# Squares on ScalarE for the upper part; from block 3 on VectorE makes the lower parts, the scalings and w_out's sums in GpSimd's place

## The chip, the cores and the metric

The kernel runs on one core of one Trainium2 chip. The metric is the device time of one execution in microseconds, from first to last instruction with what lies around it. Times below are either the median of several runs or come from one profiled execution, and the text says which.

## What is computed

A retention layer over 4 batches of 768 tokens (8 heads of 64), an MLP of 512 to 2048 to 512 with a squared ReLU, and a routed MLP of 8 experts with 384 tokens each. The inputs are float32.

```python
state = gamma * state + k_t v_t^T            # per head, over the 768 steps
y[t]  = scale * q_t state                     # 3072 tokens x 512 in all
h = x @ w_in
g = s * relu(h)**2 + b
x2 = g @ w_out
logits = x2 @ w_gate                          # 8 experts, 384 tokens each, chosen greedily
out[tokens of e] = relu(x2[tokens of e] @ w1[e]) @ w2[e]
```

The choice of experts depends on the order of the logits, so the kernel keeps more than one float32r pass of precision: each factor of a matmul is split into an upper part (rounded to float32r) and a lower part (the rest), and three products are summed (upper by upper, upper by lower, lower by upper).

## The kernel before

The tokens are cut into 12 blocks of 256 (two chunks of 128 each). The first MLP runs per block in 16 steps f over d_ff. `h_unit` (line 401) makes 12 matmuls of 256 columns into one PSUM bank (2 or 3 in turn), the h bank, and ScalarE copies relu(h) from it into the tile r (L412), which has two buffers. VectorE then multiplies max(h, 0), read from the bank, by r and writes the square in place (L413); only after this is the bank free. `r_split` (L416) has ScalarE round r to the upper part rh (L417) and, on GpSimd, subtracts to get the lower part rl (L418). `x_unit` (L421) makes six matmuls of 512 columns from rh, rl and w_out's parts (L429). `moe1` (L514) issues h units and x units in turn, x two units behind h. At the end of a block `x_out` moves the two result banks to tiles of the pool tmp (L439), which has six buffers.

The order of work on every engine is the order in which the Python code issues it; each engine takes its queue in order. `Weave.unit` (L66) issues a unit and adds its cost to a program time; before each unit it advances the side jobs (generators) whose due time has come. A side job's `yield 900` says that its next piece is due 900 ns later in program time. These numbers only set the order; nothing waits for them on the chip.

There are three stretches before the search for the experts:

- **First stage, blocks 0 to 2 together** (about 50 to 229 us of the trace): 48 units. Beside them `conv_gen` (L233) turns the weights, which come as float64, into upper and lower parts, with five VectorE operations, two ScalarE and two GpSimd operations per tile of 512 columns.
- **Blocks 3 to 9 one by one** (236 to 645 us): 16 h and 16 x units each. Beside block b runs `attn(b + 1)` (L294), the retention of the next block: per chunk `b_part` makes the scores and masks them on VectorE (am, L332), `c_part` makes the output and the next state (L345, L351, L355), ScalarE and VectorE split the output (L363, L364), and the next loads are issued on SyncE's queue. The scalings by powers of gamma (`scale_chunk`, L200: q by qdec, v by vdec) run on GpSimd one chunk ahead. Beside block 9 run the retentions of both blocks 10 and 11, with `PACE` = 0.5 for all due times. `load_dec` and `load_chunk` issue the loads.
- **Blocks 10 and 11 as a pair** (645 to 702 us): `h_pair` (L629) makes both blocks' h and their parts for each f; `l_unit` sums logits from them, and `x_last` makes the x part afterwards.

From block 3 on a further side job, `logits_gen` (L455), makes the logits of finished tokens on VectorE: `gate` (L449) issues eight operations of 512 elements that each multiply a tile by one expert's row and sum it (L452), called gates below. While no finished tile is at hand it does the same to w_out: `const_row` (L474) adds the upper and the lower part into w on GpSimd (L477), adds w to csum, also on GpSimd (L480, L482), and runs eight gates on w. `LG` gives the distance of its pieces, 900 ns of program time. `const_end` (L486) uses csum and the gates' sums once 16 rows are done.

The product that frees the bank and the two parts:

```python
        ACT.activation(r, ph, AF.Relu)
        DVE.scalar_tensor_tensor(r, ph, 0.0, r, op0=OP.max, op1=OP.mult)
        return r

    def r_split(r, rh, rl, eng=POOL):
        ACT.activation(rh, r, AF.Copy)
        eng.tensor_tensor(rl, r, rh.bitcast(F32), op=OP.subtract)
        return rh, rl
```

## Time and profile before

| | |
|---|---|
| median of 3 runs | 1163.41 us (1162.75 to 1167.41) |
| the profiled execution | 1165.52 us, span 1163.8 us |
| TensorE matmul busy | 1029.0 us (88%) |
| VectorE busy | 849.2 us (73%) |
| GpSimd busy | 424.6 us (36%) |
| ScalarE busy | 377.6 us (32%) |
| mean granted TensorE clock | 0.955 of full speed |

The profile comes from one execution; its span is the time between the first and the last recorded instruction. Busy shares are averages over stretches that have different limits, so the busy time is asked for again by stretch. A line such as L452 is a line of the kernel before; PE is TensorE, PEld its weight loads, DVE VectorE, ACT ScalarE, POOL GpSimd and SP SyncE. In the rows of busy time by stretch the columns behind PEclk are the DMA share and GB/s, and (x406) counts instructions. A block's stretch is counted here from the end of the last result copy of the block ahead (L439) to the end of its own; block 3 is counted from 236.00 us, where its first h matmuls begin. In a group's row the idle time before the group's instructions is followed by what ended it.

### The profile page before, as it was taken

How to read it: one execution, taken by the hardware profiler on the slowest of the kernel's cores; microseconds unless marked ns; L12 is line 12 of the kernel's file. 1: busy time of each engine (PE TensorE's matmuls, PEld its weight loads, DVE VectorE, ACT ScalarE, POOL GpSimd, SP SyncE). 2: the span in 40 equal slices, each digit the busy share in tenths (PEclk: the TensorE clock that was granted, in tenths of full speed). 3: DMA queues.
4: the chain of work that ended last, by engine and by line, in shares of the span. 5: the costliest groups of instructions: out<-in, count | busy, mean ns of one | idle time of the engine just before them, and what ended most of it. 6: DMA issues, size and time to landing. Idle time of an engine off the chain costs nothing.

```text
span 1163.8 us, 19793 instructions
## 1 busy us (share of the span) xinstructions
PE 1029.0 (88%) x7636; PEld 881.4 (76%) x7636; DVE 849.2 (73%) x1908; ACT 377.6 (32%) x802; POOL 424.6 (36%) x417
## 2 busy tenths in 40 slices
PE   6887787989999989999999999769789888888997
PEld 5766676878877878878888897657668676777786
DVE  3899999569989888889662724568677787967552
ACT  2333333422323322323232441123333343333442
POOL 3777787733354536454522440010211112021211
PEclk8999989989999999999999999959898999998999
DMA  9322223342212121212130000312333334243440
GB/s 332 128 89 89 96 91 111 111 145 73 65 46 64 46 64 37 74 46 65 47 95 18 20 1 1 136 55 92 118 110 104 108 106 146 79 139 118 160 139 28
DMA packets 35038, 104.50 MB, mean 90 GB/s; under 512 B 4736, under 2 KB 5248, under 8 KB 34944
## 3 DMA queue, kind: packets, MB, share of 16 engines
q1 hardware_dynamic: 30528, 89.60, 23.3%
q0 software_dynamic: 3840, 12.59, 3.3%
q8 instruction: 60, 0.98, 0.3%
q10 hardware_dynamic: 576, 1.05, 0.3%
q14 instruction: 34, 0.28, 0.1%
HBM read 90.64 MB, written 12.58 MB: 89 GB/s over the span
## 4 chain that ended last, share of the span: by engine, by line
PE 44%; DVE 31%; issue 11%; POOL 5%; DMA 5%; ACT 2%; SPq 0%; POOLq 0%; DVEq 0%; ACTq 0%
PE b L409 13%; DVE scr L452 9%; PE b L429 8%; PE b L978 7%; PE b L999 5%; PE b L653 3%; DMA big<-x2d,idx 3%; DVE r L413 3%; DVE tmp L266 3%; DVE tmp L269 2%; DVE tmp L262 2%; DVE l L956 2%; PE b L760 2%; DVE tmp L275 2%; PE b L345 2%
## 5 line engine op out<-in xcount | busy, mean ns | idle before, releaser
L452 DVE SCALAR_TENSOR_TENSOR scr<-tmp,wg 128x512 bf16<-128x512 f32 x288 | 267.3, 928 | 31.5 <-POOL tmp L477 25.1
L409 PE MATMUL b<-xh,h 128*128 128x256 f32 x704 | 205.9, 292 | 32.0 <-DVE r L413 30.3
L418 POOL TENSOR_TENSOR rl<-r,rh 128x256 fp32r<-128x256 f32 x160 | 129.9, 812 | 263.3 <-ACT rh L417 196.0
L409 PE MATMUL b<-xh,l 128*128 128x256 f32 x704 | 201.1, 286 | 0.9 <-POOL l L253 0.9
L409 PE MATMUL b<-xl,h 128*128 128x256 f32 x704 | 200.5, 285 | 0.0
L409 PEld LDWEIGHTS b<-xh,h 128*128 128x128 f32 x704 | 135.6, 193 | 50.6 <-DVE r L413 41.9
L417 ACT ACTIVATE rh<-r 128x256 fp32r<-128x256 f32 x160 | 66.9, 418 | 244.7 <-DVE r L413 244.7
L409 PEld LDWEIGHTS b<-xl,h 128*128 128x128 f32 x704 | 135.8, 193 | 3.7
L413 DVE SCALAR_TENSOR_TENSOR r<-b,r 128x256 f32<-128x256 f32 x192 | 80.4, 419 | 79.5 <-ACT r L412 78.8
L409 PEld LDWEIGHTS b<-xh,l 128*128 128x128 f32 x704 | 136.0, 193 | 1.7 <-POOL l L253 1.5
L429 PE MATMUL b<-h,rh 128*128 128x512 f32 x320 | 130.3, 407 | 5.5 <-ACT rh L417 5.4
L916 POOL DMA_INDIRECT big<-x2d,idx x24 | 26.5, 1103 | 295.2 <-issue 151.4
L429 PE MATMUL b<-h,rl 128*128 128x512 f32 x320 | 127.7, 399 | 3.2 <-POOL rl L418 2.7
L429 PE MATMUL b<-l,rh 128*128 128x512 f32 x320 | 128.8, 402 | 0.0
L412 ACT ACTIVATE r<-b 128x256 f32<-128x256 f32 x192 | 72.5, 378 | 145.5 <-PE b L409 127.5
L978 PE MATMUL b<-gh,h 128*128 128x384 f32 x256 | 94.5, 369 | 0.0
L999 PE MATMUL b<-h,hh 128*128 128x512 f32 x192 | 81.3, 423 | 13.3 <-ACT hh L981 13.3
L978 PE MATMUL b<-gl,h 128*128 128x384 f32 x256 | 89.3, 349 | 0.9 <-DVE gl L928 0.9
L978 PE MATMUL b<-gh,l 128*128 128x384 f32 x256 | 88.6, 346 | 0.0
L956 DVE TENSOR_TENSOR l<-eraw,h 128x512 fp32r<-128x512 f32 x128 | 82.3, 684 | 5.4 <-ACT h L955 5.4
L999 PE MATMUL b<-h,hl 128*128 128x512 f32 x192 | 78.6, 409 | 5.6 <-DVE hl L987 5.4
L999 PE MATMUL b<-l,hh 128*128 128x512 f32 x192 | 77.4, 403 | 0.0
(189 smaller groups left out, 2036.1 us busy)
## 6 DMA issues: line engine op xcount, KB each, us to landing
eraw<-in_w_dram SPq DMA_DIRECT2D x64, 512.0 KB, 3.5
q<-in_qkv_dram SPq DMA_DIRECT2D x36, 512.0 KB, 4.9
raw<-in_w_dram SPq DMA_DIRECT2D x32, 512.0 KB, 3.5
first<-in_qkv_dram SPq DMA_DIRECT2D x24, 256.0 KB, 5.9
qdec<-in_dec_dram SPq DMA_DIRECT2D x24, 256.0 KB, 5.6
x2d<-tmp SPq DMA_DIRECT2D x20, 256.0 KB, 6.1
wg<-in_wgT_dram SPq DMA_DIRECT2D x4, 512.0 KB, 3.8
x2d<-tmp ACTq DMA_DIRECT2D x4, 256.0 KB, 2.0
```

The costliest lines, as they stand in the source:

```text
L266: DVE.scalar_tensor_tensor(ai, hi32, -0x40000000, ai, op0=OP.bitwise_and, op1=OP.bitwise_or)
L409: PE.matmul(ph, a[:, ks], b[:, kc, :], start=(n == 0), stop=(n == 3 * KC - 1))
L412: ACT.activation(r, ph, AF.Relu)
L413: DVE.scalar_tensor_tensor(r, ph, 0.0, r, op0=OP.max, op1=OP.mult)
L417: ACT.activation(rh, r, AF.Copy)
L418: eng.tensor_tensor(rl, r, rh.bitcast(F32), op=OP.subtract)
L429: PE.matmul(X2[blk][t], a[:, ts], b, start=(f == 0 and i == 0), stop=(f == NF - 1 and i == 2))
L452: DVE.scalar_tensor_tensor(scr, x, 1.0, WG[e], op0=OP.mult, op1=OP.mult, accum_out=of[:, e:e + 1])
L653: PE.matmul(XB[c], a[:, cs], b, start=(f == 0 and i == 0), stop=(f == NF - 1 and i == 2))
L956: DVE.tensor_tensor(lo, raw[:, a, :], hi.bitcast(F32), op=OP.subtract)
L978: PE.matmul(PH[0], a[:, ks], b[:, kc, :], start=(kc == 0 and n == 0), stop=(kc == KC - 1 and n == 2))
L999: PE.matmul(Y[i, t], a[:, ts], b, start=(f == 0 and j == 0), stop=(f == NF2 - 1 and j == 2))
```

## The change

**ScalarE squares.** `r_split` now asks ScalarE for Square of r (which holds relu(h)) instead of a copy of the finished square, so the upper part no longer needs VectorE's product. `h_unit` no longer issues that product.

**Blocks 0 to 2.** `r_split` is given the bank `ph`. VectorE's product still reads the bank and still writes r in place, but it is issued behind the Square, which reads the same r, and so it waits for it. GpSimd subtracts as before.

**Block 3 on.** No product reads the bank: ScalarE's Relu alone empties it. `r_split` puts the tiles into the list `LOW`, and `low_parts` issues two VectorE operations of 128x256, r times r in place and then the subtraction. It is called at the next h unit, at the last two x units of a block, and at the end of each `h_pair`.

**Scalings.** In the blocks that are not `wide` (from the retention of block 4 on), `scale_gen` issues the two scalings on VectorE right ahead of the chunk's own scores, 1500 ns of program time apart. Before, GpSimd did it one chunk ahead. The chunks of the retentions issued as `wide` (blocks 0 to 3) keep GpSimd; one of them is the scaling of chunk 8.

**w_out's sums.** `const_row` runs its two additions on VectorE, with one further distance of 900 ns.

**Due times.** A chunk now asks for 3000 for its scalings, 1500 between the two masks, 4500 to `c_part` and 9000 behind it, 18000 in all. `PACE` is gone: the retentions of blocks 10 and 11 beside block 9 have the same distances as the others, where they had half of them.

The places where the order speaks of this are on VectorE. The first is block 4, from the mask products (L332, after the change L344) of chunk 11 on. scr is the output of a gate, wo_s its sum for w_out; before:

```order
L332 TENSOR_TENSOR am<-b_3186,mask 128x512
L332 TENSOR_TENSOR am<-b_3187,mask 128x512
L413 SCALAR_TENSOR_TENSOR r<-b_3199,r 128x256
L452 SCALAR_TENSOR_TENSOR scr,wo_s<-tmp,wg 128x512 x3
L413 SCALAR_TENSOR_TENSOR r<-b_3231,r 128x256
L452 SCALAR_TENSOR_TENSOR scr,wo_s<-tmp,wg 128x512 x3
L413 SCALAR_TENSOR_TENSOR r<-b_3263,r 128x256
L452 SCALAR_TENSOR_TENSOR scr,wo_s<-tmp,wg 128x512 x2
L364 SCALAR_TENSOR_TENSOR xl<-b_3296,xh 128x4x128
L413 SCALAR_TENSOR_TENSOR r<-b_3317,r 128x256
```

After the change:

```order
L344 TENSOR_TENSOR am<-b_3236,mask 128x512
L481 SCALAR_TENSOR_TENSOR scr,wo_s<-tmp,wg 128x512
L344 TENSOR_TENSOR am<-b_3237,mask 128x512
L447 TENSOR_TENSOR r<-r 128x256
L448 TENSOR_TENSOR rl<-r,rh 128x256
L481 SCALAR_TENSOR_TENSOR scr,wo_s<-tmp,wg 128x512
L506 TENSOR_TENSOR tmp<-h_511,l_512 128x512
L511 TENSOR_TENSOR csum<-csum,tmp 128x512
L447 TENSOR_TENSOR r<-r 128x256
L448 TENSOR_TENSOR rl<-r,rh 128x256
L481 SCALAR_TENSOR_TENSOR scr,wo_s<-tmp,wg 128x512 x2
```

The three gates and one product between two units are still three operations of `logits_gen`, of which some are now the sums of w_out (L506, L511), and the product (L413) has become a square and a subtraction (L447, L448).

The second is the end of block 9, from the masks of the last chunk (23) before the change, and from the scaling of v of chunk 22 on after it. L399 and L414 split block 11. Before:

```order
L332 TENSOR_TENSOR am<-b_6409,mask 128x512
L332 TENSOR_TENSOR am<-b_6410,mask 128x512
L413 SCALAR_TENSOR_TENSOR r<-b_6428,r 128x256
L413 SCALAR_TENSOR_TENSOR r<-b_6469,r 128x256
L413 SCALAR_TENSOR_TENSOR r<-b_6495,r 128x256
L413 SCALAR_TENSOR_TENSOR r<-b_6521,r 128x256
L399 TENSOR_TENSOR xl<-tmp,xh 128x512 x2
```

After the change:

```order
L204 TENSOR_TENSOR q_6085<-q_6085,vdec 128x512
L344 TENSOR_TENSOR am<-b_6477,mask 128x512
L344 TENSOR_TENSOR am<-b_6478,mask 128x512
L201 TENSOR_TENSOR q_6352<-q_6352,qdec 128x512
L204 TENSOR_TENSOR q_6354<-q_6354,vdec 128x512
L344 TENSOR_TENSOR am<-b_6517,mask 128x512
L344 TENSOR_TENSOR am<-b_6518,mask 128x512
L414 TENSOR_TENSOR xl<-tmp,xh 128x512 x2
L447 TENSOR_TENSOR r<-r 128x256
L448 TENSOR_TENSOR rl<-r,rh 128x256
```

Before, four products (four h units) stand between the last masks and the split, and four more between these masks and those of chunk 22. Now the masks of chunks 22 and 23 have only the scalings of chunk 23 between them, the split follows at once, and the last unit's square and subtraction come behind it.

```diff
--- before.py
+++ after.py
@@ -103,10 +103,8 @@
     SY=(5500, 5200, 4200, 3000, 2600, 1200),
     IY=(1500, 2700, 900),
     LG=(900, 880),
-    PACE=0.5,
     FE=(7110, 3450),
     FZ=(8390, 160),
-    DV=(0, 2),
     BG=(800,),
     WARM=24,
 ):
@@ -197,11 +195,13 @@
                 ts += [t[:, 0, :], t[:, 1, :]]
         QKV[j] = ts
 
-    def scale_chunk(j, eng=POOL):
-
-        eng.tensor_tensor(QKV[j][0], QKV[j][0], QD.pop(j), op=OP.mult)
-        vv = QKV[j][3].rearrange("p (a b) -> p a b", b=D)
-        POOL.tensor_tensor(vv, vv, vdec[:, j % CPB, :, None].to_broadcast([128, H, D]), op=OP.mult)
+    def scale_chunk(j, q=POOL, v=POOL):
+
+        if q:
+            q.tensor_tensor(QKV[j][0], QKV[j][0], QD.pop(j), op=OP.mult)
+        if v:
+            vv = QKV[j][3].rearrange("p (a b) -> p a b", b=D)
+            v.tensor_tensor(vv, vv, vdec[:, j % CPB, :, None].to_broadcast([128, H, D]), op=OP.mult)
 
 
     mask_f = work.tile([128, TB], F32, name="r", bufs=2)
@@ -291,7 +291,7 @@
     XF = []
     pST = [None]
 
-    def attn(blk, wide, pace=1.0):
+    def attn(blk, wide):
 
         if blk == NB - 1:
 
@@ -315,11 +315,21 @@
             if ch != CPB and ch in QD:
                 scale_chunk(ch)
 
+        def scale_gen(j):
+
+            ch = 2 * blk + j
+            if ch in QD:
+                scale_chunk(ch, DVE, None)
+                yield 1500
+                scale_chunk(ch, None, DVE)
+                yield 1500
+
         def b_part(j):
 
             if j == 0 and c0 == 0:
                 pST[0] = bank(4)
-            scale_next(j)
+            if wide:
+                scale_next(j)
             qT, kT, kt, vt = views(j)
             ps = [bank(i) for i in ((6, 7) if not wide or j == 0 else (0, 1))]
             for p in range(NP):
@@ -329,13 +339,16 @@
                               stop=True, skip_group_check=True)
             am = loads.tile([128, 2, NP, 128], F32, name="am", bufs=2)
             for s in range(2):
+                if s and not wide:
+                    yield 1500
                 DVE.tensor_tensor(am[:, s], ps[s].rearrange("p (a b) -> p a b", b=128),
                                   mask[:, None, :].to_broadcast([128, NP, 128]), op=OP.mult)
             am_of[j] = am
 
         def c_part(j):
             c = c0 + j
-            scale_next(j)
+            if wide:
+                scale_next(j)
             am = am_of.pop(j)
             qT, kT, kt, vt = views(j)
             py = bank((5, 2)[j] if wide else 5)
@@ -373,16 +386,18 @@
                 load_chunk(ch)
 
         for j in range(2):
-            b_part(j)
+            if not wide:
+                yield from scale_gen(j)
+            yield from b_part(j)
             if wide:
                 yield 1500
                 if j:
                     c_part(0)
                     yield 2500
             else:
-                yield 7600 * pace
+                yield 4500
                 c_part(j)
-                yield 10400 * pace
+                yield 9000
         if wide:
             c_part(1)
             yield 2500
@@ -399,6 +414,7 @@
             DVE.tensor_tensor(xl[:, ps], XF[i], xh[:, ps].bitcast(F32), op=OP.subtract)
 
     def h_unit(blk, f, hb):
+
         xh, xl = XT[blk]
         wh, wl = W[2 * f]
         ph = bank(hb)[:, 0:TB]
@@ -410,13 +426,26 @@
                 n += 1
         r = work.tile([128, TB], F32, name="r", bufs=2)
         ACT.activation(r, ph, AF.Relu)
-        DVE.scalar_tensor_tensor(r, ph, 0.0, r, op0=OP.max, op1=OP.mult)
-        return r
-
-    def r_split(r, rh, rl, eng=POOL):
-        ACT.activation(rh, r, AF.Copy)
-        eng.tensor_tensor(rl, r, rh.bitcast(F32), op=OP.subtract)
+        return r, ph
+
+    LOW = []
+
+    def r_split(r, rh, rl, ph=None):
+
+
+        ACT.activation(rh, r, AF.Square)
+        if ph is None:
+            LOW.append((r, rh, rl))
+        else:
+            DVE.scalar_tensor_tensor(r, ph, 0.0, r, op0=OP.max, op1=OP.mult)
+            POOL.tensor_tensor(rl, r, rh.bitcast(F32), op=OP.subtract)
         return rh, rl
+
+    def low_parts():
+        while LOW:
+            r, rh, rl = LOW.pop(0)
+            DVE.tensor_tensor(r, r, r, op=OP.mult)
+            DVE.tensor_tensor(rl, r, rh.bitcast(F32), op=OP.subtract)
 
     def x_unit(blk, f, xb, ts=(0, 1)):
         if f == 0 and 0 in ts:
@@ -474,12 +503,13 @@
     def const_row(f):
         wh, wl = W[2 * f + 1]
         w = tmp.tile([128, 512], F32, name="tmp")
-        POOL.tensor_tensor(w, wh.bitcast(F32), wl.bitcast(F32), op=OP.add)
+        DVE.tensor_tensor(w, wh.bitcast(F32), wl.bitcast(F32), op=OP.add)
         yield LG[0]
         if f == 0:
-            POOL.tensor_copy(csum, w)
+            DVE.tensor_copy(csum, w)
         else:
-            POOL.tensor_tensor(csum, csum, w, op=OP.add)
+            DVE.tensor_tensor(csum, csum, w, op=OP.add)
+        yield LG[0]
         yield from gate(w, wo_s[:, f])
         CONST.append(f)
 
@@ -522,14 +552,17 @@
                 def hu(n=n):
                     f, i = seq[n]
                     conv_until(2 * f + 1)
-                    r = h_unit(blks[i], f, 2 + n % 2)
+                    low_parts()
+                    r, ph = h_unit(blks[i], f, 2 + n % 2)
                     R2[blks[i], f] = r_split(r, work.tile([128, TB], F32R, name="rh", bufs=3),
                                              work.tile([128, TB], F32R, name="rl", bufs=3),
-                                             DVE if len(blks) > 1 and n % DV[1] < DV[0] else POOL)
+                                             ph if len(blks) > 1 else None)
                 units.append((1320, hu))
             if n >= lag:
                 def xu(n=n - lag):
                     f, i = seq[n]
+                    if n + lag >= len(seq):
+                        low_parts()
                     x_unit(blks[i], f, xbs[i])
                     if f == NF - 1:
                         x_out(blks[i])
@@ -575,7 +608,7 @@
     wv.add(tail)
     def attn2():
         for b in (NB - 2, NB - 1):
-            yield from attn(b, False, PACE)
+            yield from attn(b, False)
 
     for blk in range(3, NB - 2):
         nxt = Side(attn(blk + 1, False) if blk < NB - 3 else attn2())
@@ -629,11 +662,12 @@
     def h_pair(f):
         rs = []
         for i, blk in enumerate(pair):
-            wv.unit(1320, lambda: rs.append(h_unit(blk, f, 2 + i)))
+            wv.unit(1320, lambda: rs.append(h_unit(blk, f, 2 + i)[0]))
 
         R4[f] = [wpool.tile([128, 512], F32R, name=f"{p}{2 * f}", tag=f"{p}{2 * f}") for p in "hl"]
         for i, r in enumerate(rs):
             r_split(r, *(t[:, i * TB:(i + 1) * TB] for t in R4[f]))
+        low_parts()
 
     def l_unit(f):
         for i, r in enumerate(R4[f]):
```

## Rows read from the trace of the kernel before

**Rows 1.** Busy time, blocks 3 to 9: us, PE, PEld, DVE, ACT, POOL, PEclk.
```profile
236.00:295.04 59.04, 56.00 (x406) 49.60 (x406) 48.38 (x112) 17.30 (x42) 20.81 (x23) 0.94 0.31 97
295.04:352.36 57.32, 53.69 (x390) 46.39 (x388) 49.10 (x109) 15.38 (x38) 26.28 (x27) 1.00 0.18 56
352.36:407.12 54.76, 52.77 (x398) 46.28 (x396) 48.53 (x106) 16.36 (x41) 28.13 (x27) 1.00 0.18 59
407.12:467.20 60.08, 55.14 (x406) 48.54 (x404) 53.04 (x111) 16.47 (x40) 30.85 (x29) 0.97 0.16 49
467.20:524.74 57.54, 54.02 (x390) 46.28 (x388) 47.23 (x110) 15.04 (x39) 28.31 (x27) 1.00 0.19 60
524.74:582.93 58.19, 55.21 (x406) 48.29 (x404) 45.75 (x103) 16.37 (x42) 28.06 (x28) 0.97 0.18 56
582.93:644.54 61.61, 60.90 (x504) 54.64 (x501) 28.76 (x67) 19.74 (x49) 17.93 (x24) 1.00 0.18 54
```

**Rows 2.** VectorE in block 5: count, busy us, mean ns, idle before.
```profile
L452 DVE SCALAR_TENSOR_TENSOR scr<-tmp,wg 128x512 bf16<-128x512 f32 x42 | 41.4, 986 | 5.1 <-POOL tmp L477 4.2
...
L413 DVE SCALAR_TENSOR_TENSOR r<-b,r 128x256 f32<-128x256 f32 x16 | 6.7, 418 | 1.1 <-ACT r L412 0.9
...
L332 DVE TENSOR_TENSOR am<-b,mask 128x512 f32<-128x512 f32 x4 | 2.6, 678 | 0.0
```

**Rows 3.** Timeline of VectorE, 332 to 341 us: start, length, engine, line.
```profile
332.59 1.66 DVE L452 SCALAR_TENSOR_TENSOR scr<-tmp,wg 128x512 bf16<-128x512 f32 x1
...
335.11 0.67 DVE L452 SCALAR_TENSOR_TENSOR scr<-tmp,wg 128x512 bf16<-128x512 f32 x1
...
335.83 1.17 DVE L452 SCALAR_TENSOR_TENSOR scr<-tmp,wg 128x512 bf16<-128x512 f32 x1
```

**Rows 4.** Timeline of GpSimd, 329 to 342 us.
```profile
331.90 1.80 POOL L482 TENSOR_TENSOR csum<-csum,tmp 128x512 f32<-128x512 f32 x1
...
335.72 0.73 POOL L418 TENSOR_TENSOR rl<-r,rh 128x256 fp32r<-128x256 f32 x1 [2.02 <-ACT rh L417]
```

**Rows 5.** All gates (line 452): count, ns min/median/max.
```profile
L452 DVE SCALAR_TENSOR_TENSOR scr<-tmp,wg x288: 673/693/1668, 236.6 to 661.2; 128x512 bf16<-128x512 f32 x144
```

**Rows 6.** Waits, 400 to 580 us: us in total, times, longest.
```profile
PE b L409 <- DVE r L413: 7.1, 5, 3.7
```

**Rows 7.** TensorE, 330 to 352 us: starts of two h groups.
```profile
339.35 0.28 PE L409 MATMUL b<-xh,h 128*128 128x256 f32 x1
...
342.17 0.28 PE L409 MATMUL b<-xh,h 128*128 128x256 f32 x1
```

**Rows 8.** Timeline, 612 to 636 us: attention of one chunk.
```profile
616.74 1.09 PE L345 MATMUL b<-am,q 128*64 128x128 f32 x16
...
618.22 1.16 PE L355 MATMUL b<-q,sbd 128*128 128x128 f32 x8
...
619.42 0.66 ACT L361 ACTIVATE tmp<-b 128x256 f32<-128x256 f32 x2 [1.23 <-PE b L355]
...
624.96 1.16 PE L328 MATMUL b<-q 64*128 64x128 f32 x16
```

**Rows 9.** Groups of the whole kernel, from the page.
```profile
L956 DVE TENSOR_TENSOR l<-eraw,h 128x512 fp32r<-128x512 f32 x128 | 82.3, 684 | 5.4 <-ACT h L955 5.4
```

**Rows 10.** Groups of ScalarE in the first stage (50 to 226 us).
```profile
L417 ACT ACTIVATE rh<-r 128x256 fp32r<-128x256 f32 x48 | 20.1, 418 | 100.1 <-DVE r L413 100.1
...
L239 ACT ACTIVATE tmp<-raw 128x512 f32<-128x512 f32 x27 | 18.0, 666 | 6.6 <-POOL l L253 6.6
```

**Rows 11.** Waits in the first stage (50 to 226 us).
```profile
ACT rh L417 <- DVE r L413: 100.1, 48, 4.2
...
DVE r L413 <- ACT r L412: 11.3, 8, 2.4
```

**Rows 12.** Timeline, 639 to 646 us: the split of the last block.
```profile
641.00 1.14 ACT L398 ACTIVATE xh<-tmp 128x512 fp32r<-128x512 f32 x2
...
641.65 1.65 DVE L399 TENSOR_TENSOR xl<-tmp,xh 128x512 fp32r<-128x512 f32 x2 [1.00 <-ACT xh L398]
```

## Prediction

> **What bounds the kernel now.** I read the page's first two parts (busy shares, 40 slices), then the busy time block by block, then one block's VectorE groups, the waits and the timeline. The change touches only what runs up to about 700 us; the search and the second MLP behind it are not edited, so I price that part at nothing and look at three stretches.
>
> Blocks 3 to 9 take 59.04, 57.32, 54.76, 60.08, 57.54, 58.19 and 61.61 us [rows 1]. How much of that is TensorE? One unit, an h group and an x group, takes 342.17 - 339.35 = 2.82 us when nothing waits [rows 7], so 16 units are 45.1 us. A chunk of attention is 1.16 us for the score matmuls and, from the first matmul of L345 to the end of L355, 618.22 + 1.16 - 616.74 = 2.64 us [rows 8]; two chunks are 7.6. TensorE alone would need **52.7 us a block**. Blocks 4 to 8 take 287.9 in all, 24.4 more than five times that. Block 9 has four chunks (45.1 + 15.2 = 60.3) and takes 61.6: it is TensorE's.
>
> What holds blocks 4 to 8 is VectorE. In block 5 (54.76 us) it is busy 48.5 [rows 1], and of the 6.2 us in which it is idle 4.2 are a wait for the sum of w_out's parts that GpSimd makes [rows 2]. TensorE in turn waits for VectorE's product that frees the h bank (7.1 us in 180) [rows 6]. The gate row tells why VectorE is so full: 42 gates of 986 ns each in block 5 [rows 2], where the median gate of the kernel takes 693 and the longest 1668 [rows 5]. The long ones stand beside GpSimd's work. The gate that starts at 332.59 takes 1.66 us while GpSimd's sum runs from 331.90 to 333.70; the one at 335.83 takes 1.17 beside GpSimd's subtraction from 335.72 to 336.45; the one between them, with GpSimd idle, takes 0.67 [rows 3, 4]. In each case the gate ends about 0.55 us after GpSimd does: it is held, then runs. Sixteen subtractions a block at 1.17 - 0.69 = 0.48 and six operations for w_out's sums at up to 1.66 - 0.69 = 0.97 come to 13.5 us, about what the block's gates have too much.
>
> **Blocks 4 to 8, VectorE's sum, on block 5's 54.8 us.**
> - Taken away: the held time of the gates, since GpSimd has no work left in these blocks: 42 x (986 - 693) ns = 12.3 us [rows 2, 5]; the wait for GpSimd's sum, 4.2; the products that emptied the bank, 16 x 418 ns = 6.7 [rows 2].
> - Added: two operations of 128x256 a unit, the square and the subtraction. No row shows this form. The nearest below is the product of the same size, 418 ns [rows 2]; above, a subtraction of the same kind at twice the width, 684 ns [rows 9]. I take 0.42, the same size counting most: 32 x 0.42 = 13.4 us (21.9 at the upper end). The Trainium skill (VectorE: DVE Perf Modes, The TRN2 errata) gives an fp32 `tensor_tensor` (N + 151) cycles at 0.96 GHz; by that an estimate for 256 columns is 424 ns, which would make the term 13.6, and for 512 columns it says 691 where the row has 684. Three rows of w_out's sums, two operations each at 684 ns [rows 9]: 4.1. Two chunks' scalings, four operations at 684: 2.7.
> - Together 54.8 - 12.3 - 4.2 - 6.7 + 13.4 + 4.1 + 2.7 = **51.8 us**, just under TensorE's 52.7.
>
> So the bound changes hands. The two streams are nearly level, and a little is lost whenever one waits for the other, so I take 53.0 a block: 287.9 - 265.0 = **-22.9 us**. What hides VectorE's lateness is the lag of two units between h and x: rl is needed only after another x, h, x and h, some 5.6 us. That cover is thin at the end of a block, where h has run out and only two x groups follow.
>
> **Block 3** has the same work without w_out's sums, but the clock there is 0.94 [rows 1]. I keep most of the clock's part (0.06 x 59 = 3.5 us) and the lost start, and take -3.5 (from 59.0 to 55.5).
>
> **Block 9** loses its even pace. The attention of blocks 10 and 11 was spread at half the distances over block 9; now each chunk asks for 18 us of program time where the block has about 42, so two chunks (22 and 23) are issued in one piece before the last two x groups. The order shows it: four mask products with only scalings between them, the split of block 11, and only then the last lower part. Twice TensorE then waits for two masks, 2 x 678 ns [rows 2] and a hand-over: 1.5 us each. Behind the last chunk stand ScalarE's copies (0.66 us [rows 8]), its split and VectorE's subtractions. The split starts 0.65 us before the subtractions, which take 1.65 [rows 12]; with the lower part (0.84) that is 0.66 + 0.65 + 1.65 + 0.84 = 3.8 us, of which an x group (about half a unit, 1.4 [rows 7]) and a third of the next (two matmuls of six) cover 1.8: 2.0 us bare. Sum **+5.0 us**. The loads of q, k and v move with the chunks; SyncE issues each a whole chunk ahead, behind stores that wait for gates, and the chunk's 18 us hide it, so I cost it at nothing; if the gates were late by that much, the load would be late next.
>
> **The first stage (blocks 0 to 2).** Here VectorE still empties the bank and GpSimd still makes rl. What is new is that VectorE's product, which writes r in place, must wait for ScalarE's Square as well as for Relu. A Square lies between the copy's 418 ns at the same width and the 666 ns of a Square at twice the width [rows 10]; I take 0.45 with the hand-over. It costs only where VectorE is ready early: 8 waits for Relu among 48 products [rows 11]. Eight times 0.45 is 3.6; some fall where TensorE has slack, so **+2.0**. The bounds are 0 and 48 x 0.45 = 21.6. ScalarE itself no longer waits for VectorE there; VectorE is the one that is full, so I give nothing for that.
>
> **Blocks 10 and 11.** Sixteen gates, 0.72 us from one to the next [rows 3], and four small operations a pair (1.7) come to 20 us in the first five pairs. TensorE needs two h groups of half a unit each [rows 7] and two matmuls, by the same row some 0.2 each, so 5 x 3.2 = 16. The two r buffers take up some 3 us of that lateness, an estimate: **+1.0**.
>
> **Sum.** -22.9 - 3.5 + 5.0 + 2.0 + 1.0 = -18.4 us. The profiled execution took 1165.5 us (span 1163.8), 2.1 above the median of the runs shown; the sum makes it 1147.1, and the median 1163.4 becomes **1145 us**.
>
> **Rivals.**
> 1. *VectorE is late where the cover is thin* (no change, 0.11). The lower parts stand in one queue with three gates a unit. If each block ends with VectorE 4 us late, x waits there, and blocks stay near 57: 285 for the five, -3, block 3 -1; with +8 elsewhere that is about 1167. For it: 51.8 and 52.7 leave no reserve, and a wait of VectorE for Relu or for a score bank holds everything behind it. Against: in block 5 VectorE idled for other things than GpSimd for only 2 us.
> 2. *The gates stay long* (slower, 0.08). The place is VectorE's queue in blocks 4 to 8. If the 986 ns were the gate's own price, or the new operations cost 684, VectorE would have 51.8 + 12.3 = 64.1 or 51.8 + 8.5 = 60.3 us a block. The point from which it decides is 57.6, today's mean: an excess of 5.8 us, that is less than half of the 12.3 coming back or small operations above 0.60 us. At 62, five blocks are 310, +22, and with +8 the time is about 1193. Against it stands the pairing of long gates with GpSimd's rows [rows 3, 4]. The Trainium skill (Perfetto Trace Analysis, Optimizing Scalar/DVE Operations) points this way with its advice that work may be moved from a saturated DVE to Scalar or even GPSIMD, the reverse of this change. It adds that the two share an SBUF read port, so that offloading between them might not help; no row here tells against that addition.
> 3. *The Square delays every product of the first stage* (no change, 0.03). "ScalarE empties the h bank" is not done there: the product still reads it. If VectorE arrived before the Square in all 48 units, 21.6 us in place of 2.0 would give 1165. Against it: ScalarE's copy waits for VectorE's product 48 times of 48, 100.1 us in all, and VectorE for ScalarE 8 times [rows 11].
> 4. *More than forecast* (0.06): blocks at 52.7, block 3 at 53, 2 us in block 9, nothing in the first stage: -28, which is 1135.
>
> **Numbers.** Forecast 0.72. Half a per cent, about what a measurement of this kernel can tell from no change, is 5.8 us: below 1157.6 is faster, above 1169.2 slower. Faster 0.78 (forecast and rival 4), same 0.14 (rivals 1 and 3), slower 0.08 (rival 2). The range for 8 in 10: low, five blocks at 52.7 (-24.4), block 3 -6, block 9 +2 gives 1135, and 1133 if block 3's clock stays up all through. High: blocks at 55 (-13), block 3 -2, block 9 +6, first stage +3, blocks 10 and 11 +1 gives 1158; 1160 takes in the near end of rival 1, so that some 0.2 stays outside.
>
> **What would show it.** Right: GpSimd almost empty from block 4 on; a mean gate near 700 ns in block 5; no wait of VectorE for w; blocks 4 to 8 at 52 to 54 us with TensorE's waits for the h bank gone; new waits of TensorE for the masks and the last lower part near the end of block 9, some 5 us; the small operations at 0.42. Wrong: gates still near 0.95, small operations above 0.6, a first stage more than 4 us longer, or x groups waiting for rl in the middle of blocks.

## The result and the profile after

The changed kernel takes **1144.8 us** (median of 4 runs, 1142.75 to 1146.4) against 1163.28 for the kernel before (also 4 runs): a ratio of 0.9833, 95% interval 0.9805 to 0.986. The forecast was 1145. The profiled execution took 1142.75 us (span 1141.0); it is the fastest of its four, while that of before took 1165.52, some 2 us over the median, so stage differences between the two profiles add up to 22.8 us and the medians differ by 18.5.

Busy time in blocks 3 to 9, one row each; the columns are those of [rows 1], but block 3 is counted here from the end of the first stage. Counted so, block 3 of the kernel before is the row ahead of the seven:

```profile
229.13:295.04 65.91, 62.33 (x510) 55.26 (x508) 51.65 (x117) 19.16 (x46) 23.92 (x26) 0.95 0.35 108
```

```profile
231.07:291.87 60.80, 59.57 (x504) 53.48 (x501) 52.28 (x139) 19.18 (x46) 4.67 (x4) 1.00 0.36 113
291.87:344.40 52.53, 52.53 (x386) 47.16 (x386) 48.60 (x131) 16.06 (x38) 0.00 (x0) 1.00 0.20 61
344.40:396.56 52.16, 52.16 (x394) 46.82 (x394) 48.27 (x129) 16.70 (x41) 0.00 (x0) 1.00 0.19 61
396.56:449.64 53.08, 53.08 (x402) 47.73 (x402) 48.95 (x131) 16.70 (x41) 0.00 (x0) 1.00 0.20 61
449.64:502.97 53.33, 52.62 (x386) 47.17 (x386) 48.51 (x131) 16.06 (x38) 0.00 (x0) 1.00 0.20 60
502.97:555.13 52.16, 52.16 (x394) 46.82 (x394) 48.96 (x131) 16.71 (x40) 0.20 (x1) 1.00 0.19 62
555.13:621.56 66.43, 62.70 (x514) 55.87 (x514) 42.18 (x109) 20.27 (x51) 1.22 (x4) 1.00 0.18 54
```

The second to sixth of the seven are blocks 4 to 8: TensorE is busy all the time in four of the five, GpSimd has one operation of 0.2 us in all, and VectorE, which now does more, is busy for 243.3 us in the five together where [rows 1] adds up to 243.7. The last row is block 9, with 3.7 us in which TensorE idles.

VectorE's groups in block 5 (count, busy us, mean ns, idle before), which answer to [rows 2]:

```profile
L481 DVE SCALAR_TENSOR_TENSOR scr<-tmp,wg 128x512 bf16<-128x512 f32 x41 | 28.2, 688 | 0.7
L448 DVE TENSOR_TENSOR rl<-r,rh 128x256 fp32r<-128x256 f32 x16 | 6.8, 425 | 1.4
L447 DVE TENSOR_TENSOR r<-r 128x256 f32<-128x256 f32 x16 | 6.7, 419 | 0.3 <-ACT rh L436 0.3
...
L344 DVE TENSOR_TENSOR am<-b,mask 128x512 f32<-128x512 f32 x4 | 2.7, 684 | 0.0
```

A gate takes 688 ns on the mean where it took 986, and each new small operation takes 0.42 us, as taken.

**The stages.** Each is counted between ends of result copies (line 439 before, 468 after), the pair (blocks 10 and 11) to the start of VectorE's first addition to the last four chunks' logits (line 695 before, 729 after), all from one profile of each kernel, in us. The rows from the third on are the experiments of the next section:

| | first stage ends | block 3 | blocks 4 to 8 | block 9 | pair | rest | span |
|---|---|---|---|---|---|---|---|
| before | 229.13 | 65.91 | 287.89 | 61.61 | 59.64 | 459.62 | 1163.8 |
| after | 231.07 | 60.80 | 263.26 | 66.43 | 60.03 | 459.41 | 1141.0 |
| bank only | 229.13 | 67.27 | 275.45 | 61.22 | 66.62 | 460.21 | 1159.9 |
| product kept | 229.48 | 60.90 | 263.79 | 66.00 | 59.81 | 458.52 | 1138.5 |
| the same again | 230.10 | 60.88 | 263.78 | 66.00 | 59.81 | 464.13 | 1144.7 |
| half distances | 232.08 | 60.80 | 263.32 | 64.23 | 60.02 | 462.95 | 1143.4 |
| first stage as before | 227.81 | 60.63 | 263.30 | 66.47 | 60.37 | 458.52 | 1137.1 |
| lower part alone | 229.31 | 62.44 | 283.90 | 62.38 | 59.80 | 463.57 | 1161.4 |
| sums and scalings alone | 227.13 | 66.07 | 269.49 | 61.61 | 59.65 | 460.65 | 1144.6 |
| GpSimd reads | 229.32 | 64.41 | 280.93 | 66.70 | 60.36 | 457.88 | 1159.6 |
| GpSimd writes | 230.09 | 61.37 | 264.14 | 66.52 | 61.89 | 458.79 | 1142.8 |
| product kept, half | 227.38 | 60.90 | 263.75 | 65.44 | 59.85 | 458.88 | 1136.2 |
| GpSimd's work alone | 227.84 | 68.12 | 267.18 | 62.38 | 59.79 | 460.79 | 1146.1 |
| block 9 as before | 227.85 | 60.88 | 263.80 | 62.89 | 59.87 | 461.21 | 1136.5 |

The two rows of the same code (product kept, and the same again) differ by 0.03 us in blocks 3 to 9 together, and by 6.2 in the span: the first stage and the long rest vary between executions, the blocks hardly. So the blocks' columns tell kernels apart to a few tenths, the rest does not.

### The profile page after: what moved, and what is told of

It reads as the page before. It is cut to its first block, busy times and chain, and to the rows that moved or that the text cites. A ratio compares the mean times of both kernels' runs of the same rounds, so it can differ in the third digit from the quotient of the medians.

```text
span 1141.0 us, 19761 instructions
## 1 busy us (share of the span) xinstructions
PE 1016.3 (89%) x7636; PEld 875.8 (77%) x7636; DVE 875.2 (77%) x2114; ACT 385.1 (34%) x802; POOL 221.7 (19%) x211
## 4 chain that ended last, share of the span: by engine, by line
PE 55%; DVE 23%; issue 11%; DMA 5%; ACT 2%; POOL 2%; SPq 0%; POOLq 0%; DVEq 0%; ACTq 0%
PE b L425 17%; PE b L458 13%; PE b L1012 6%; PE b L1033 5%; PE b L687 3%; DVE tmp L262 3%; DMA big<-x2d,idx 3%; DVE l L990 2%; PE b L794 2%; PE b L358 2%; PE b L368 2%; DVE tmp L266 2%; PE b L338 2%; DVE tmp L269 2%; DVE cmp L787 2%
## 5 line engine op out<-in xcount | busy, mean ns | idle before, releaser
L425 PE MATMUL b<-xh,h 128*128 128x256 f32 x704 | 201.7, 287 | 22.6 <-DVE r L440 20.9
L481 DVE SCALAR_TENSOR_TENSOR scr<-tmp,wg 128x512 bf16<-128x512 f32 x288 | 198.3, 689 | 6.8 <-ACT tmp L468 1.8
L447 DVE TENSOR_TENSOR r<-r 128x256 f32<-128x256 f32 x144 | 60.7, 421 | 25.6 <-ACT h L436 17.9
L1015 ACT ACTIVATE hh<-b 128x384 fp32r<-128x384 f32 x64 | 31.3, 489 | 138.3 <-PE b L1012 138.3
L458 PEld LDWEIGHTS b<-h,rl 128*128 128x128 f32 x320 | 61.0, 191 | 19.3 <-DVE rl L448 5.5
```

The lines of the kernel that those rows point to most:

```text
L425: PE.matmul(ph, a[:, ks], b[:, kc, :], start=(n == 0), stop=(n == 3 * KC - 1))
L447: DVE.tensor_tensor(r, r, r, op=OP.mult)
L458: PE.matmul(X2[blk][t], a[:, ts], b, start=(f == 0 and i == 0), stop=(f == NF - 1 and i == 2))
L481: DVE.scalar_tensor_tensor(scr, x, 1.0, WG[e], op0=OP.mult, op1=OP.mult, accum_out=of[:, e:e + 1])
L1015: ACT.activation(hh, PH[0], AF.Relu)
```

## The experiments

A ratio below is the time of a run's kernel over that of the kernel before, with its 95% interval.

**Theory:** blocks 4 to 8 were long because GpSimd's rows held VectorE's gates. **Rivals:** the h bank came free too late; or the lower part reached the x groups too late through GpSimd.

**1. Only the bank is freed earlier.** The kernel before; from block 3 on no product reads the bank, ScalarE squares, and GpSimd makes the square and the lower part.

```diff
-        DVE.scalar_tensor_tensor(r, ph, 0.0, r, op0=OP.max, op1=OP.mult)
+        if blk < 3:
+            DVE.scalar_tensor_tensor(r, ph, 0.0, r, op0=OP.max, op1=OP.mult)
...
-        ACT.activation(rh, r, AF.Copy)
-        eng.tensor_tensor(rl, r, rh.bitcast(F32), op=OP.subtract)
+        ACT.activation(rh, r, AF.Square if square else AF.Copy)
+        if square:
+            POOL.tensor_tensor(r, r, r, op=OP.mult)
+        POOL.tensor_tensor(rl, r, rh.bitcast(F32), op=OP.subtract)
```

> The kernel before with one part of the change: from block 3 on ScalarE's Relu alone empties the h bank and ScalarE squares for the upper part; the square and the lower part are made by GpSimd, which keeps the scalings and w_out's sums. Theory (the gain is GpSimd's work taken from beside the gates): GpSimd gets 16 more operations a block, each holding a gate for up to 0.48 us (7.7 us), and VectorE loses 16 products (6.7 us), so VectorE's sum stays near 55.8 us a block and blocks 4 to 8 stay at 55 to 58; time 1158 to 1172 us, mean gate in block 5 at 1.0 us or more. Rival (the gain is the h bank that no longer waits for VectorE): blocks 4 to 8 at 52 to 53.5, time 1140 to 1149.

Measured: 1160.31 us, ratio 0.9979 (0.9958 to 1.0). Blocks 4 to 8 are 12.4 us shorter, the pair is 7.0 longer (GpSimd makes its lower parts too), block 3 is 1.4 longer. Groups in block 5:

```profile
L455 DVE SCALAR_TENSOR_TENSOR scr<-tmp,wg 128x512 bf16<-128x512 f32 x43 | 46.0, 1071 | 5.6 <-POOL tmp L480 4.2
...
L421 POOL TENSOR_TENSOR rl<-r,rh 128x256 fp32r<-128x256 f32 x16 | 16.9, 1057 | 1.3
L420 POOL TENSOR_TENSOR r<-r 128x256 f32<-128x256 f32 x16 | 14.0, 875 | 5.7 <-ACT rh L418 5.7
```

The gates are longer than ever (1071 ns), and yet the blocks are shorter: in blocks 4 to 8 TensorE waited 9.9 us for VectorE's product before, and waits here for GpSimd's rl alone, 9.6 us, so a late VectorE costs less.

**2. GpSimd is emptied, the bank is not freed earlier.** The changed kernel with the product and the copy as before.

```diff
+        DVE.scalar_tensor_tensor(r, ph, 0.0, r, op0=OP.max, op1=OP.mult)
         return r, ph
...
-        ACT.activation(rh, r, AF.Square)
+        ACT.activation(rh, r, AF.Copy)
...
-            DVE.tensor_tensor(r, r, r, op=OP.mult)
```

> The changed kernel with one part undone: VectorE's product empties the h bank everywhere as before, ScalarE copies its result, and from block 3 on VectorE subtracts; scalings and w_out's sums stay on VectorE, GpSimd has nothing from block 4 on. Theory (held gates): VectorE's sum is the same as in the changed kernel, since the product takes the place of r times r, and the gates run at 0.69; blocks 4 to 8 at 52 to 54.5 us, time 1139 to 1149. Rival (the bank): TensorE waits for the product behind three gates, blocks 4 to 8 at 56 to 58, time 1156 or more.

Measured: 1139.88 us, ratio 0.9803 (0.9758 to 0.9849). Blocks 4 to 8 are 24.1 us shorter, nearly as much as with the whole change (24.6). So the bank's release was a way around the late VectorE, and once VectorE is no longer late it is worth half a microsecond. This run keeps the new order and distances of the attention; without them GpSimd's emptying is worth less (experiment 6).

**3. Which of GpSimd's work?** The kernel before with the subtraction for rl alone on VectorE (a unit later), and with w_out's sums and the scalings alone.

```diff
-        eng.tensor_tensor(rl, r, rh.bitcast(F32), op=OP.subtract)
+        if late:
+            LOW.append((r, rh, rl))
...
+            DVE.tensor_tensor(rl, r, rh.bitcast(F32), op=OP.subtract)
```

> The kernel before, with one part of the change alone: from block 3 on the subtraction that makes the lower part rl runs on VectorE, one unit later; the product still empties the h bank, scalings and w_out's sums stay on GpSimd. Theory (GpSimd's rows hold VectorE's gates, and each kind of row holds its share): the 16 subtractions no longer hold gates (16 x 0.48 = 7.7 us a block less), and cost 16 x 0.42 = 6.7 us themselves, so VectorE's 54.8 us in block 5 becomes 53.8; the mean gate there falls from 986 to about 800 ns, w_out's sums still hold some; blocks 4 to 8 at 54 to 56.5 us, time 1150 to 1158. Rival (the lower parts' path through GpSimd to the x groups is what cost the time): TensorE's idle time is gone from these blocks, they come to 53.5 or less, time 1147 or less. A third: no gain at all (1161 or more), the parts only work together.

```diff
-                scale_chunk(ch)
+                scale_chunk(ch, POOL if wide else DVE)
...
-        POOL.tensor_tensor(w, wh.bitcast(F32), wl.bitcast(F32), op=OP.add)
+        DVE.tensor_tensor(w, wh.bitcast(F32), wl.bitcast(F32), op=OP.add)
...
-            POOL.tensor_tensor(csum, csum, w, op=OP.add)
+            DVE.tensor_tensor(csum, csum, w, op=OP.add)
```

> The kernel before, with the other part alone: w_out's two sums per row run on VectorE, and the scalings of the retentions from block 4 on too, one chunk ahead as before; the subtraction for rl stays on GpSimd and the product empties the bank. Theory (each kind of GpSimd row holds gates): out of VectorE's 54.8 us in block 5 go the wait for the sum (4.2), the holds of the sums (5.8) and of the scalings (about 4 x 0.97 = 3.9), in come 4.1 and 2.7 for the operations: 47.7 us. Gates still held by 16 subtractions: a mean of about 0.86 us. Blocks 4 to 8 at 52.7 to 54.5, time 1143 to 1150. Rival (the 16 subtractions are the part that matters, as they are the most): blocks at 56 or more, time 1155 or more.

Measured: the lower part alone 1158.36 us, ratio 0.9972 (0.9954 to 0.9989), 0.4 us over what was expected, blocks 4 to 8 at 56.8 each, a little over it, and the mean gate of block 5 at 879 ns where about 800 was expected; sums and scalings alone 1147.12, ratio 0.9868 (0.9837 to 0.99), blocks at 53.9, as expected, though VectorE is busy for 51.48 us in block 5 and not for 47.7. In blocks 4 to 8 they give 4.0 and 18.4 us, together 22.4 where the same two edits at once give 20.7 (experiment 6). The few long rows of GpSimd cost more than the 16 short ones a block; how much of that is held gates, and how much VectorE's waiting for the sum, is not separated. In the run with the lower part alone the new subtraction is itself held by the rows that stay on GpSimd, while the product that reads the bank is not (all in block 5, ns min/median/max):

```profile
L429 DVE TENSOR_TENSOR rl<-r,rh x16: 411/419/1500, 352.3 to 403.8; 128x256 fp32r<-128x256 f32 x16
...
L413 DVE SCALAR_TENSOR_TENSOR r<-b,r x16: 409/416/425, 351.3 to 402.2; 128x256 f32<-128x256 f32 x16
```

**4. What holds a gate?** The changed kernel, where GpSimd does something useless for each h unit of blocks 3 to 9: either an operation that reads SBUF or three memsets, each into the rl tile that VectorE then overwrites.

```diff
+                    if len(blks) == 1:
+                        POOL.tensor_tensor(rl.rearrange("p (a b) -> p a b", b=128),
+                                           mask[:, None, :].to_broadcast([128, 2, 128]),
+                                           mask[:, None, :].to_broadcast([128, 2, 128]), op=OP.mult)
```

> The changed kernel, with GpSimd made busy for nothing: in blocks 3 to 9 each h unit has GpSimd multiply a constant tile by itself into the rl tile, which VectorE then overwrites (128x256, reads SBUF, about 0.7 to 0.9 us, 16 a block). No result uses it. Theory (GpSimd's instructions that read SBUF hold VectorE's two-input operations until they end): gates beside them lengthen by 0.5 to 0.9 us, the mean gate in block 5 goes from 688 ns to 0.85 to 1.0 us; VectorE's 48.3 us busy come to 56 or more, blocks 4 to 8 to 55 to 60, time 1156 to 1180. Rival (nothing was held; the gates were long because of their order or of waits that GpSimd's results caused): gates at 0.69, time 1143 to 1149.

```diff
+                    if len(blks) == 1:
+                        for _ in range(3):
+                            POOL.memset(rl.bitcast(F32), 0.0)
```

> The same place, the same tile and the same waits as in the run with reads, but GpSimd only writes: three memsets of 128x256 per h unit, together about 0.8 us. Theory (only GpSimd instructions that read SBUF hold VectorE): gates stay at 0.69 to 0.72 us, blocks 4 to 8 at 52 to 53.6, time 1143 to 1149. Rival (any GpSimd instruction on SBUF holds VectorE, or the additional semaphores cost it): as with the reads, gates at 0.85 or more, time 1156 or more.

Measured: with reads 1166.93 us, ratio 1.0029 (1.0011 to 1.0047), all of the gain gone (in its profile, the fastest of its ten runs, blocks 4 to 8 take back 17.7 of the 24.6 us and block 3 3.6); with writes 1146.88, ratio 0.9871 (0.9843 to 0.9899). Block 5 with reads, then with writes:

```profile
L481 DVE SCALAR_TENSOR_TENSOR scr<-tmp,wg 128x512 bf16<-128x512 f32 x41 | 31.1, 759 | 0.7
L448 DVE TENSOR_TENSOR rl<-r,rh 128x256 fp32r<-128x256 f32 x16 | 8.6, 539 | 1.7
...
L559 POOL TENSOR_TENSOR rl<-mask 128x256 fp32r<-128x256 bf16 x16 | 11.7, 729 | 43.1 <-PE b L458 34.0 <-DVE r L447 5.2 <-DVE scr L481 3.9
```

```profile
L481 DVE SCALAR_TENSOR_TENSOR scr<-tmp,wg 128x512 bf16<-128x512 f32 x41 | 28.2, 688 | 0.7
L448 DVE TENSOR_TENSOR rl<-r,rh 128x256 fp32r<-128x256 f32 x16 | 6.8, 425 | 2.0
...
L560 POOL MEMSET rl<- 128x256 f32 x49 | 15.3, 313 | 37.4 <-PE b L458 35.5
```

With writes GpSimd is busy for longer (15.3 us against 11.7) and the two VectorE rows do not change at all. So it is the reading that holds, in the same place with the same semaphores. The Trainium skill (SBUF — State Buffer, Who interferes with whom) says that a DVE instruction with two SBUF inputs contends with a GpSimd instruction that reads SBUF, not with one that only writes; both runs agree, and so does the product above, which has one input in PSUM and never exceeds 425 ns. From the timeline with reads (start, length), GpSimd first:

```profile
359.45 0.61 POOL L559 TENSOR_TENSOR rl<-mask 128x256 fp32r<-128x256 bf16 x1 [2.21 <-PE b L458]
...
366.77 1.03 POOL L559 TENSOR_TENSOR rl<-mask 128x256 fp32r<-128x256 bf16 x1 [2.20 <-PE b L458]
```

```profile
366.63 0.69 DVE L481 SCALAR_TENSOR_TENSOR scr<-tmp,wg 128x512 bf16<-128x512 f32 x1
...
367.37 0.98 DVE L481 SCALAR_TENSOR_TENSOR scr<-tmp,wg 128x512 bf16<-128x512 f32 x1
```

The gate that began ahead of GpSimd's row (366.63) keeps its 0.69 us, and GpSimd's row behind it takes 1.03 where the one at 359.45 takes 0.61; the next gate, begun while GpSimd runs, takes 0.98. In this pair whoever comes second is held. The trace of the kernel before, counted over blocks 4 to 8, says the same of every gate: the 94 that begin while GpSimd is at work take 716 to 1668 ns, and each ends 0.55 us after GpSimd does; the 117 others take 673 to 694 ns. The expectation of the run with reads missed two numbers: the mean gate is 759 ns and not 850 or more, and VectorE is busy for 52.4 us and not 56; still each block is 3.5 us longer. Subtractions are held too (539 ns on the mean of 16), so VectorE is busy for 52.41 us of 54.77 beside TensorE's 52.49: the two streams are level, and TensorE waits 2.3 us of this block for VectorE's rl.

**5. The first stage.** The changed kernel, with a copy and the order of before in blocks 0 to 2: the product is issued right behind Relu, and ScalarE rounds its result.

```diff
         ACT.activation(r, ph, AF.Relu)
+        if blk < 3:
+            DVE.scalar_tensor_tensor(r, ph, 0.0, r, op0=OP.max, op1=OP.mult)
...
-        ACT.activation(rh, r, AF.Square)
+        ACT.activation(rh, r, AF.Square if ph is None else AF.Copy)
```

> The changed kernel with blocks 0 to 2 as before (product behind Relu, ScalarE copies its result). Theory: the Square in front of the product costs the first stage 2 us; its end falls from 231.1 to 229.1 us, time 1142 to 1144. Rival (the 2 us come from another place, such as the instruction order on ScalarE by chance): the end stays at 231, time 1144 to 1146.

Measured: 1140.99 us, ratio 0.9814 (0.977 to 0.9858), which the time alone cannot tell from the change; the first stage ends at 227.8, and both are some 1 us below what was expected. By the table: ten profiles without the Square there end the first stage at 227.1 to 230.1, 228.5 on the mean; four with it at 229.3 to 232.1, mean 230.6. The two groups overlap; by their means the Square costs about 2 us.

**6. Block 9.** First half distances for blocks 10 and 11 (a factor 0.5 on each `yield`), in the changed kernel and in the one with the product kept.

```diff
-            yield from attn(b, False)
+            yield from attn(b, False, 0.5)
```

> The changed kernel with the due times of the last two retentions halved again. Theory: the flush before the last two x groups is gone, block 9 falls from 66.4 to 61 to 62.5 us, time 1139.5 to 1142. Rival (block 9 is longer because VectorE has four chunks' scalings and const_end there, not because of the flush): block 9 stays above 65, time 1143 to 1146.

> The changed kernel with the product that empties the h bank kept as before (no Square anywhere) and with half distances for the retentions of blocks 10 and 11 beside block 9. Theory: the bank need not be freed, so blocks 4 to 8 stay at 264 us; the first stage ends at 228 to 229.5, as before the change; block 9 at 63.5 to 64.5, two us less than with full distances. Time 1136 to 1139, below both kernels. Rival (the two savings don't add up, the kept product holds block 9): block 9 at 66, time 1140 or more.

Measured: 1143.12 us, ratio 0.9821 (0.9776 to 0.9866), block 9 at 64.2, not at 62; and 1140.48, ratio 0.9812 (0.9793 to 0.9831), block 9 at 65.4, so both kernels missed their time and their block. The distances are not what matters most: the waits for whole masks are gone, but TensorE now waits ahead of scores, which begin as soon as the scaling right ahead of them is done. In the changed kernel with half distances (VectorE, then TensorE):

```profile
570.59 0.69 DVE L201 TENSOR_TENSOR q<-q,qdec 128x512 f32<-128x512 f32 x1
```

```profile
571.37 1.16 PE L338 MATMUL b<-q 64*128 64x128 f32 x16 [0.70 <-issue]
...
585.84 1.16 PE L338 MATMUL b<-q 64*128 64x128 f32 x16 [0.64 <-PE b L425]
```

These two waits are 1.3 of the 2.0 us in which TensorE idles in that block; with the product kept as well, such waits are 2.0 of 3.1. Next the kernel before with GpSimd's three kinds of work moved and nothing else (the two edits of 3 together):

> The kernel before with only GpSimd's three kinds of work moved to VectorE from block 3 on (the subtraction for rl a unit later, w_out's sums, the scalings one chunk ahead as before) and nothing else: the product empties the bank, the attention's order and distances are those of before. Theory (what the change gains is GpSimd being empty; what it loses in block 9 is the new distances with whole masks of two chunks in one piece): blocks 4 to 8 at 262 to 266 us in all, block 3 at 60 to 62, the first stage at 227 to 229.5, block 9 at 61 to 63 as before, time 1133 to 1138, the fastest of all. Rival (block 9 is longer because VectorE now has the lower parts at its end, whatever the distances): block 9 at 65 or more, time 1139 or more.

Measured: 1148.65 us, ratio 0.9879 (0.9858 to 0.99), against 1133 to 1138 expected. Block 9 is at 62.4, as the theory said, but block 3 takes 68.1 instead of 61, and blocks 4 to 8 take 267.2, 20.7 less than before but 3.4 more than with the product kept in the new order; TensorE waits 3.5 us there for VectorE's rl. The timeline of that run in block 3 (VectorE, then TensorE, then the busy time of the stretch) shows why block 3 is long:

```profile
239.83 0.69 DVE L202 TENSOR_TENSOR q<-q,qdec 128x512 f32<-128x512 f32 x1 [3.83 <-DMA q<-in_qkv_dram]
...
242.91 0.41 DVE L413 SCALAR_TENSOR_TENSOR r<-b,r 128x256 f32<-128x256 f32 x1
```

```profile
243.38 0.58 PE L409 MATMUL b<-xh,h 128*128 128x256 f32 x1 [4.80 <-DVE r L413]
243.76 0.42 PE L409 MATMUL b<-xl,h 128*128 128x256 f32 x1
243.97 0.41 PE L409 MATMUL b<-xh,l 128*128 128x256 f32 x1
...
248.48 0.28 PE L409 MATMUL b<-xh,h 128*128 128x256 f32 x1
248.59 0.28 PE L409 MATMUL b<-xl,h 128*128 128x256 f32 x1
```

```profile
239.19:250.55 11.36, 7.17 (x33) 6.56 (x34) 7.91 (x20) 2.29 (x6) 0.00 (x0) 0.70 0.13 51
```

Scaled one chunk ahead, q is not there yet: VectorE waits 3.83 us for its load, with the product that frees the bank behind it, and TensorE idles 4.80. After that idle time its matmuls start 0.21 us apart, and from 248.48 on 0.11 to 0.12: the granted clock of this stretch is 0.70, a mixture of 1.2 and 2.4 GHz. The wait of 4.8 us and the slow matmuls behind it (an estimate: half of the 5.1 us from 243.38 to 248.48) make up block 3's 7.2. So the scaling right ahead of its chunk, part of the change, is what block 3 needs, and block 9 is where it costs. The last kernel uses each where it helps: the product kept, GpSimd emptied, and for blocks 10 and 11 alone the order and distances of before, with scalings one chunk ahead.

```diff
+        old = blk >= NB - 2
...
-                if s and not wide:
+                if s and not (wide or old):
...
-                yield 4500
+                yield 3800 if old else 4500
                 c_part(j)
-                yield 9000
+                yield 5200 if old else 9000
```

> The kernel with the product kept and GpSimd emptied, with one thing changed: the retentions of blocks 10 and 11 beside block 9 have the distances of before (3800 and 5200), both masks in one piece, and scalings one chunk ahead, on VectorE. Blocks 3 to 8 keep the new order, with scalings right ahead of their chunk. Theory (the new order helps block 3, where a scaling one chunk ahead waits for its load and holds the product behind it, and costs block 9 some 4 us): block 3 at 60 to 62, blocks 4 to 8 at 264, block 9 at 62 to 63.5; time 1135 to 1138, some 3.5 us below the kernel with the product kept, measured beside it. Rival (block 9 grows whatever the distances, since block 8 hands over work): block 9 at 65 or more, the same time as the other.

> The kernel with the product kept once more, only to stand beside the run with the old distances in block 9 on the same chip: 1138 to 1141.

Measured: **1136.68 us**, ratio 0.9785 (0.9754 to 0.9817), the lowest median of all; the one with the product kept beside it 1142.95, ratio 0.983 (0.98 to 0.986), 2 us over its expectation (and over the 1139.88 of the same code in experiment 2). No run of the one reaches the other's, so this kernel is the faster of these two. The changed kernel was not run beside it, and its interval (0.9805 to 0.986) overlaps. The two profiles differ by 8.2 us, of which 3.1 lie in block 9; the others lie in the first stage and the rest, and are put down to the variation of executions.

```profile
227.85:288.73 60.88, 59.54 (x504) 53.44 (x501) 51.28 (x139) 19.20 (x47) 4.37 (x4) 1.00 0.36 112
552.53:615.42 62.89, 62.46 (x514) 55.51 (x514) 41.27 (x109) 20.22 (x52) 0.87 (x4) 1.00 0.19 57
```

The rows are its blocks 3 and 9: the clock is 1.00 in both, and TensorE idles 0.4 us in block 9. Distances, masks and scalings were set back together here, so their shares are not separated.

## Why the prediction was right, step by step

- **Blocks 4 to 8** (forecast -22.9, measured -24.6). The mechanism is shown by experiments 2 to 4. TensorE idled 17.1 us in these blocks by [rows 1] and idles 0.7 after; the other 8.3 us are a shorter busy time, some of it work that slipped into block 9 and matmuls at full clock in blocks 6 and 8, where [rows 1] had 0.97. VectorE's sum of 51.8 was too high: it is busy for 48.27 us in block 5. Its base, 54.8, was the whole block, with 2.0 us in which VectorE idled for other reasons; the rest is one gate fewer (41) and records that overlap. With a reserve of 4 us instead of 1, the 0.3 us a block put down for waiting did not arise.
- **The small operations** were taken at 0.42 us and took 0.419 and 0.425. The estimate by the Trainium skill's formula that the prediction quotes, 0.424, agrees. The upper end of 0.684 is out.
- **Block 3** (forecast -3.5, measured -5.1 from the end of the first stage on). The forecast counted from 236.00 us; the first h matmul begins at 236.75 there and at 238.84 after, and counted from these the block goes from 58.3 to 53.0, as in rival 4. The clock's part came: 1.00 where it was 0.95, and TensorE is busy 2.8 us less. The step left out TensorE's one long wait of 2.7 us for GpSimd's late rl, which is 0.2 after; idle time falls from 3.6 to 1.2 us.
- **Block 9** (forecast +5.0, measured +4.8): the sum was right by luck, its parts were not. TensorE idles 3.7 us instead of 0.7, so +3.0, and has 1.8 us more work, which slipped in from block 8 (`const_end`'s eight matmuls begin at 587.65, before at 576.70 and so in block 8; the first scores begin inside the block, before 0.8 us ahead of it). The timeline of the end of the block after the change:

```profile
607.41 1.29 DVE L344 TENSOR_TENSOR am<-b,mask 128x512 f32<-128x512 f32 x2 [2.87 <-PE b L338]
...
608.20 1.53 PE L358 MATMUL b<-am,q 128*64 128x128 f32 x15 [0.82 <-issue]
...
612.51 1.29 DVE L344 TENSOR_TENSOR am<-b,mask 128x512 f32<-128x512 f32 x2 [2.62 <-PE b L338]
...
613.30 1.64 PE L358 MATMUL b<-am,q 128*64 128x128 f32 x16 [0.82 <-ACT sbd L383]
...
617.28 1.29 DVE L414 TENSOR_TENSOR xl<-tmp,xh 128x512 fp32r<-128x512 f32 x2 [3.48 <-ACT xh L413]
...
618.07 0.79 POOL L638 TENSOR_TENSOR strict<-mask,ident 128x128 bf16<-128x128 bf16 x1 [86.27 <-DMA ident<-in_cst_dram]
618.49 0.65 DVE L447 TENSOR_TENSOR r<-r 128x256 f32<-128x256 f32 x1
...
619.17 0.42 DVE L448 TENSOR_TENSOR rl<-r,rh 128x256 fp32r<-128x256 f32 x1
...
619.65 0.50 PE L458 MATMUL b<-h,rl 128*128 128x512 f32 x1 [1.79 <-DVE rl L448]
```

  The masks cost TensorE 0.8 us twice, not 1.5, because the output's matmuls start after the first of the two; the last lower part costs 1.8 as against 2.0. That step's cause, the two chunks in one piece, is part of it: with half distances these waits are gone, but the scores wait for the scalings right ahead of them, which no step named. With the order of before (last kernel) only the slipped work is left, 62.9 against 61.6.
- **First stage** (+2.0): 1.9 between the two profiles, 2.1 over all. The size came; the mechanism is not shown. VectorE waits 6 times, 11.2 us in all, for the Square, where by [rows 11] it waited 8 times, 11.3 us, for Relu; TensorE waits 32.1 us for the product instead of 31.0. Where the rest is lost stays open.
- **Blocks 10 and 11** (+1.0): +0.4.
- **Rivals.** VectorE late at block ends: from 400 to 555 us TensorE waits for rl once, 0.7 us. Gates that stay long: 688 ns. The advice of the Trainium skill quoted there would have cost time here: the kernel before has the work on GpSimd, and blocks 4 to 8 take 24.6 us more. The Trainium skill's addition on the shared read port agrees with the runs with reads and with writes. The Square before every product: 6 waits, not 48. More than forecast: blocks 4 to 8 and block 3 did come out as in that case, block 9 and the first stage as forecast.

By the steps alone the forecast was 4.4 us too cautious against the two profiles (-18.4 against -22.8). That the medians meet within 0.2 us is in part luck: executions of one kernel vary by some 6 us outside the blocks.

## What to carry to other kernels

Before work goes to GpSimd to relieve VectorE, look at what each of its instructions reads: a GpSimd row that reads SBUF lengthens VectorE's operations with two SBUF inputs beside it, and a mean duration well above the median of the same group is the sign. When such a kernel also has an early wait that looks like the bottleneck (here the h bank), test the two apart: in blocks 4 to 8 freeing the bank alone gave 12.4 of 24.6 us and lost most of it elsewhere, emptying GpSimd alone gave 20.7, and with the new order of the attention 24.1. An operation moved from an idle engine into a full queue takes its own wait along: a scaling that could wait for its load on GpSimd stalls the product behind it on VectorE.

## What was not expected of the hardware

- VectorE's square of one tile by itself (r times r) is held as well: 0.65 us instead of 0.42 beside GpSimd's row that reads two tiles (618.07 to 618.86 above), though both inputs are the same tile. In blocks 4 to 8 of the run with reads (ns min, median, max) the longest takes 881, where without GpSimd's rows it takes 426:

```profile
L447 DVE TENSOR_TENSOR r<-r x80: 409/418/881, 296.2 to 571.7; 128x256 f32<-128x256 f32 x80
```

- The hold works in both directions: GpSimd's row of 0.61 us took 1.03 behind a running gate. Of its 80 rows in blocks 4 to 8 of that run 28 take 0.61 us and 52 take longer, up to 1.15; each of the 52 began while VectorE ran an operation with two SBUF inputs, and ends 0.47 us after that.
- Over the 80 products of blocks 4 to 8 before, which read one input from the bank, none took over 426 ns, with GpSimd busy for half of that time (min, median, max in ns):

```profile
L413 DVE SCALAR_TENSOR_TENSOR r<-b,r x80: 406/419/426, 299.0 to 576.6; 128x256 f32<-128x256 f32 x80
```
